# Windowed attention and SwiGLU on one core: attention after the first tile by four heads, in array quadrants

## The chip, the cores and the metric

The kernel runs on one core of a Trainium2 chip. A core has a TensorE (PE, matmuls), a VectorE (DVE), a ScalarE (ACT), a GpSimd (POOL) and a SyncE (SP); the last issues DMAs, and GpSimd and ScalarE issue some too. The metric is the device time of one execution in microseconds, the median of several. A profile is one execution more, taken with the hardware profiler; its span runs from the first instruction to the last.

## The reference

Eight batches of eight heads, 576 positions, 64 elements a head. Each position attends to itself and the 63 before it. The result, 4608 tokens of 512, goes through a SwiGLU block of width 1536.

```python
scores = scale * np.matmul(q, k.transpose(0, 1, 3, 2))        # scale = 1/8
rel = pos[:, None] - pos[None, :]
mask = (rel >= 0) & (rel < 64)
attn = softmax(np.where(mask, scores, -1e9))
x = np.matmul(attn, v)            # heads side by side: (4608, 512)
g = x @ w_gate
out = (g / (1 + np.exp(-g)) * (x @ w_val)) @ w_out
```

Inputs and the output are float32; the kernel computes in bfloat16 with float32 sums.

## The kernel before

**Tiles.** Nine tiles of 512 tokens. Tiles 0 to 6 and 8 are the first 512 positions of a batch; tile 7 (`LAST`) collects the last 64 positions of all eight batches. In a tile of the first kind the keys fall into eight blocks of 64, and a block of 64 queries needs two of them: its own and the one before. In tile 7 each batch has one block of queries and two blocks of keys.

**Pairs.** A pair `u` is two heads. `qT` and `kT` hold a pair's transposed queries and keys, 64 partitions a head, four pairs in four slots. `scores` computes keys by queries: for key block `j`, one matmul per head, 64 deep (a head's elements), 64 wide (the block's keys), over the queries of blocks `j` and `j + 1`, 128 columns. The result goes to partitions 64 (j mod 2) and on of `s_ps`, so even and odd key blocks lie in two partition halves of 512 columns, one PSUM bank a head. Queries of block 0 have no block before; a matmul with the tile `zero` fills that place. ScalarE takes the exponential of 128 x 1024 into `E`, and VectorE multiplies with a 0/1 mask. (In tile 0 a bias matmul in the accumulation does the masking.)

`totals` multiplies `E` with ones, 128 deep, so that both key halves are summed, a head on each column half. ScalarE forms the reciprocal as exp(-ln(sum)). `mix` multiplies with v: per query block and head one matmul, 128 deep (both key blocks), 64 wide, over 64 columns. For that v must exist in two arrangements, since a query block's two key blocks stand in the two halves in either order: `v1` as loaded and `v2`, shifted by 64 positions. The shift is done by VectorE for tiles 0 and 1 (`shift_pair`) and by DMAs of SyncE after that (`shift_v` with `shift_dma`). `scale` multiplies with the reciprocal into `xT`.

**The loop.** For each tile `t` from 2 on, TensorE's order, which is the order of the code, is: scores of pairs 0 and 1; the output projection of rows `s = 0` of the tile before; scores of pairs 2 and 3; sums of pairs 0 and 1; projections 1 and 2; sums of pairs 2 and 3; all products (`mix_all`); projection 3; then twelve SwiGLU blocks (`gate_value`), 8 matmuls of 128 x 128 x 512 each. A projection is 12 matmuls of that size. Tile 1 does its attention between the columns of tile 0's projection (`columns`). VectorE transposes the next tile's queries and keys between the blocks (`turn`, with L192 and L202), in order with the products of the SwiGLU blocks (L326).

**PSUM.** Two double-bank buffers (`ps_a`) hold scores, then attention outputs; two banks `g` and two banks `v` (`ps_f`) hold gates and values, projections (`g`) and sums (`v`).

**Loads.** GpSimd's queue brings weights and, two tiles ahead, queries and keys with a cast to bfloat16 (`load_qk`: four loads `q_s`, sixteen `k_s`, L87 and L107). v comes over SyncE as float32 (`stage_v`, four DMAs, one buffer) and GpSimd casts it (`cast_v`, L148); for tiles 1 and 2 GpSimd's queue loads it with the cast (L128). A load on GpSimd's queue waits until the one eight before it has landed; SyncE's DMAs have eight such places too. GpSimd's order around tile 1 is: a third of the gate weights, `q_s` of tile 1, two thirds of `wo`, four loads of v, the last third of `wo`, and the loads of tile 2. SyncE stores the output rows (`project_end`), then shifts v, then loads the next float32 v.

Of the kernel before, what the change touches and what calls it, by code (L numbers as in the profile page):

```python
# [8 lines left out]
P = 128  # L9
# [8 lines left out]
def kernel(  # L18
# [22 lines left out]
    epool = ctx.enter_context(tc.tile_pool(name="epool", bufs=7))  # L41
# [9 lines left out]
    v1 = [cst.tile([P, 4, H, D], BF16, name=f"v1{i}") for i in range(2)]  # L51
    v2 = [cst.tile([P, 4, H, D], BF16, name=f"v2{i}") for i in range(2)]
# [3 lines left out]
    zero = cst.tile([P, 64], BF16, name="zero")  # L56
    bias = cst.tile([P, 2, 4, 4, 2, 16], BF16, name="bias")
    mask = cst.tile([P, 2, 16, 4, 2, 4], BF16, name="mask")
    maskl = cst.tile([P, 2, 16, 8, 4], BF16, name="maskl")
# [66 lines left out]
    def load_v(eng, dst, t, which=range(4)):  # L126
        for i in which:
            eng.dma_start(  # L128
                dst[:, i], v[batch(t), :, P * i:P * i + P].rearrange("h r d -> r h d")
            )  # L130

    def load_last_v():
        for b in range(8):
            nc.gpsimd.dma_start(
                (v1, v2)[b // 4][LAST % 2][:, b % 4],
                v[b, :, S - P:S].rearrange("h r d -> r h d"),
            )

    def new_v(t):
        staged[t, "v"] = stage.tile([P, 4, H, D], FP32, name="v_f", tag="v", bufs=1)  # L140

    def stage_v(t):
        new_v(t)
        load_v(nc.sync, staged[t, "v"], t)

    def cast_v(t, which=range(4), copy=nc.gpsimd.tensor_copy):
        for i in which:
            copy(v1[t % 2][:, i], staged[t, "v"][:, i])  # L148

    def shift_pair(t, u):  # L150
        hs = slice(2 * u, 2 * u + 2)
        a, b = v1[t % 2][:, :, hs], v2[t % 2][:, :, hs]
        nc.vector.tensor_copy(b[64:128, 1:4], a[64:128, 0:3])
        nc.vector.tensor_copy(b[0:64], a[0:64])

    def shift_v(t, copy, lo=0, hi=4):

        a, b = v1[t % 2], v2[t % 2]
        top = min(hi, 3)
        if top > lo:  # L160
            copy(b[64:128, lo + 1:top + 1], a[64:128, lo:top])
        copy(b[0:64, lo:hi], a[0:64, lo:hi])
# [44 lines left out]
    def scores(t, u):  # L207

        qT = queries[t][:, u, :]
        E = epool.tile([P, 2, 512], BF16, name="E", tag="E")  # L210
        s_ps = ps_a.tile([P, 2, 512], FP32, name="s_ps", tag="a")
        if t == LAST:
            pieces = [
                (c, b, b + 1, kT[t % 2 if b < 4 else 2], P * (b % 4) + 64 * c)
                for b in range(8) for c in range(2)
            ]
        else:
            pieces = [(1, 0, 1, None, 0)] + [
                (j % 2, j, min(8, j + 2), kT[t % 2], 64 * j) for j in range(8)
            ]  # L220
        if t < TURNED:
            for c in range(2):
                for h in range(2):
                    r = slice(64 * h, 64 * h + 64)
                    nc.tensor.matmul(
                        s_ps[64 * c:64 * c + 64, h], identb[r, r],
                        bias[r, c ^ h].rearrange("r e i c x -> r (e i c x)"),
                        start=True, stop=False,
                    )
        for c, lo, hi, src, x in pieces:  # L230
            for h in range(2):
                r = slice(64 * h, 64 * h + 64)
                nc.tensor.matmul(  # L233
                    blocks(s_ps[64 * c:64 * c + 64, h], t, lo, hi),
                    zero[r] if src is None else src[r, u, x:x + 64],
                    blocks(qT[r], t, lo, hi),
                    start=t >= TURNED, stop=t >= TURNED or (lo > 5 and src is not None),
                )
        nc.scalar.activation(E[:], s_ps[:], AF.Exp, scale=0.125)  # L239
        if t >= TURNED:  # L240
            nc.vector.tensor_mul(  # L241
                E[:].rearrange("r h x -> r (h x)"),
                E[:].rearrange("r h x -> r (h x)"),
                maskl[:].rearrange("r h e b x -> r (h e b x)") if t == LAST
                else mask[:].rearrange("r h e i c x -> r (h e i c x)"),
            )
        weights[t, u] = E

    def totals(t, u, d_ps):
        for h in range(2):  # L250
            nc.tensor.matmul(  # L251
                d_ps[64 * h:64 * h + 64], ones[:, 0:D], weights[t, u][:, h, :]
            )

# [9 lines left out]
    def sums(t, u, d_ps):  # L264
        totals(t, u, d_ps)
        r = room(1)[:, 0]
        log(r, d_ps)
        invert(r)
        inverse[t, u] = r

    def mix(t, u, o_ps):
        E = weights.pop((t, u))
        for m in range(8):
            for h in range(2):
                nc.tensor.matmul(  # L275
                    blocks(o_ps[64 * h:64 * h + 64], t, m, m + 1),
                    (v1, v2)[m // 4][t % 2][:, m % 4, 2 * u + h, :] if t == LAST
                    else (v2, v1)[m % 2][t % 2][:, m // 2, 2 * u + h, :],
                    blocks(E[:, h, :], t, m, m + 1),
                )  # L280

# [5 lines left out]
    def values(t, u, o_ps):  # L287
        mix(t, u, o_ps)
        scale(t, u, o_ps)
# [7 lines left out]
    def finish_values(t):  # L297
        for u in (2, 3):
            sums(t, u, d_tile())
        mix_all(t)  # L300

    def mix_all(t):
        tiles = wide("ao_ps"), wide("ao_ps")
        for u in range(4):
            mix(t, u, tiles[u // 2][:, u % 2])
        for u in range(4):
            scale(t, u, tiles[u // 2][:, u % 2])
# [86 lines left out]
    new_v(0)  # L394
# [4 lines left out]
    load_v(nc.sync, staged[0, "v"], 0, (0, 1))  # L399
# [4 lines left out]
    nc.vector.memset(zero[:], 0.0)  # L404
    for i in range(2):
        nc.vector.memset(v2[i][64:128, 0], 0.0)
# [10 lines left out]
    for a in range(2):  # L417
        half = tri[64 * a:64 * a + 64]
        nc.gpsimd.affine_select(
            out=half[:, 1 - a], in_=half[:, 1 - a], compare_op=ALU.is_ge, fill=0.0,  # L420
            base=-1, pattern=[[-1, 64]], channel_multiplier=1,
        )
        nc.gpsimd.affine_select(
            out=half[:, a], in_=half[:, a], compare_op=ALU.is_ge, fill=0.0,
            base=0, pattern=[[1, 64]], channel_multiplier=-1,
        )
# [45 lines left out]
    load_v(nc.gpsimd, v1[0], 0, (2, 3))  # L472
    keep_warm(1)
    scores(0, 0)
# [4 lines left out]
    scores(0, 1)  # L479
# [17 lines left out]
    load_v(nc.gpsimd, v1[1], 1)  # L497
    weights_o(8, 12)
    cast_v(0, (0, 1), on_v)
    scores(0, 2)  # L500
    turn_pe(3)
    d_ps, r = wide("d_ps"), room(2)
    for u in range(2):
        totals(0, u, d_ps[:, u])
        inverse[0, u] = r[:, u]
    log(r, d_ps[:])
    invert(r)
    scores(0, 3)

    def log_of(u):  # L510
        d_ps = one("d_ps")
        totals(0, u, d_ps)
        inverse[0, u] = room(1)[:, 0]
        log(inverse[0, u], d_ps)
# [3 lines left out]
    for u in range(2):  # L518
        shift_pair(0, u)
    for u in range(2):  # L520
        values(0, u, ps_f.tile([P, 512], FP32, name="ao_ps", tag="gv"[u])[:])
    for u in (2, 3):
        shift_pair(0, u)
# [7 lines left out]
    for u in (2, 3):  # L531
        values(0, u, one("ao_ps"))
# [3 lines left out]
    for m in range(12):  # L536
# [4 lines left out]
        if m == 2:  # L541
            for i in range(4):
                nc.vector.tensor_copy(
                    mask[:, 0, :, i], tri[:].rearrange("r c (x e) -> r e c x", e=16)
                )
            nc.vector.memset(mask[64:128, 0, :, 0, 0, :], 0.0)
            nc.vector.tensor_copy(mask[:, 1], mask[:, 0])
# [18 lines left out]
    for u in range(4):  # L566
        scores(1, u)
        if u == 1:
            columns(0, 4)
    columns(4, 7)  # L570
    for u in (0, 2):
        d_ps, r = wide("d_ps"), room(2)
        for i in range(2):
            totals(1, u + i, d_ps[:, i])
            inverse[1, u + i] = r[:, i]
        log(r, d_ps[:])
        invert(r)
    load_qk(2)
    load_v(nc.gpsimd, v1[0], 2)
    for u in range(4):  # L580
        shift_pair(1, u)
# [6 lines left out]
    for t in range(1, NT):  # L588
        if t > 1:
            set_exp()  # L590
            for u in range(4):
                scores(t, u)
                if u == 1:
                    project(t - 1, 0)
            for u in range(2):
                sums(t, u, d_tile())
            for s in (1, 2):
                project(t - 1, s)
            finish_values(t)
# [4 lines left out]
        elif t + 1 < NT:  # L604
            if t > 1:
                cast_v(t + 1)
            shift_v(t + 1, shift_dma)
# [4 lines left out]
        if t == 2:  # L612
# [4 lines left out]
            for b in range(8):  # L617
                nc.gpsimd.tensor_copy(
                    maskl[:, 0, :, b], tri[:, 1].rearrange("r (x e) -> r e x", e=16)
                )  # L620
            nc.gpsimd.tensor_copy(maskl[:, 1], maskl[:, 0])
# [39 lines left out]
```

## Time and profile before

| | |
|---|---|
| Median of 3 runs | 333.98 us (332.97 to 335.63) |
| Profiled execution | span 331.9 us, 2.0 us under that median |
| TensorE clock granted | 0.997 |
| TensorE matmuls | 2743, busy 324.5 us |
| VectorE, ScalarE, GpSimd busy | 211.3, 168.6, 139.8 us |
| exp of scores (L239) | 36 of 128 x 1024, 1020 ns each |
| mask product (L241) | 28 of 128 x 1024 bf16, 709 ns each |
| log, invert (L259, L262) | 30 each of 128 x 512, 590 and 630 ns |
| scores (L233), sums (L251), products (L275) | 704, 72 and 576 matmuls recorded |

How to read the lines below: a timeline row has the start in us from the span's first instruction, the length in us, the engine, the line of the code, the operation, output <- inputs, for a matmul rows*columns of the array that it takes, the shape of the moving operand, and the number of instructions that the row merges. What stands in brackets is how long the engine had been idle before it and what ended that. A matmul's length includes its way through the array, so neighbouring rows overlap; the distance of starts is what it costs. "POOL" rows of DMAs show the issue, not the transfer.

### The profile page before, as it was taken

The numbers are of one execution on the slowest core, as the hardware profiler recorded it, in microseconds if no ns is written. First come the engines' busy times: TensorE is split into PE (matmuls) and PEld (weight loads), VectorE is DVE, ScalarE is ACT, GpSimd is POOL, SyncE is SP. The second block draws the span as 40 slices with busy tenths as digits, with TensorE's granted clock in tenths as the row PEclk, the third lists the DMA queues.
The fourth block names the chain that finished last, engine by engine and source line by source line (L and its number), as shares of the span: only waits on it lengthen the run. The fifth ranks groups of instructions, "written<-read, shape, count | busy, mean of one in ns | idle before, by whom it ended". The sixth has DMA issues, their size and how long they took to land.

```text
span 331.9 us, 6997 instructions
## 1 busy us (share of the span) xinstructions
PE 324.5 (98%) x2743; PEld 154.6 (47%) x2743; DVE 211.3 (64%) x325; ACT 168.6 (51%) x239; POOL 139.8 (42%) x249
## 2 busy tenths in 40 slices
PE   8899999999999999999999999999999999999995
PEld 4444444444544454445444444444444544454443
DVE  5855756586576856875668566856785586754431
ACT  5855556338533853377336743565347533953310
POOL 4944535846848985457024986263200000000000
PEclk9999999999999999999999999999999999999998
DMA  7999999999999779859922999199401320010013
GB/s 258 188 196 202 203 190 201 152 192 219 185 236 179 89 136 253 140 80 218 191 58 32 171 203 140 17 199 181 97 0 41 89 55 2 24 73 33 2 34 95
DMA packets 83249, 43.59 MB, mean 131 GB/s; under 512 B 63888, under 2 KB 77968, under 8 KB 83216
## 3 DMA queue, kind: packets, MB, share of 16 engines
q0 software_dynamic: 50416, 23.08, 56.4%
q1 hardware_dynamic: 31776, 19.02, 21.0%
q10 hardware_dynamic: 1024, 1.05, 1.1%
q8 instruction: 21, 0.34, 0.4%
q14 instruction: 12, 0.10, 0.1%
HBM read 54.00 MB, written 9.44 MB: 191 GB/s over the span
## 4 chain that ended last, share of the span: by engine, by line
PE 87%; DMA 8%; POOL 3%; issue 0%; SPq 0%; DVE 0%; POOLq 0%
PE o_ps L341 28%; PE g_ps L332 25%; PE v_ps L332 25%; DMA k_r<-in_k_dram 4%; DMA wo<-in_moe_w_out_dram 3%; PE s_ps L233 3%; PE d_ps L251 3%; PE ao_ps L275 2%; DMA q_f<-in_q_dram 1%; POOL wg L166 1%; POOL wv L166 1%; PE o_ps L377 1%; POOL v L128 1%; POOL qk_b L450 0%; SPq L73 0%
## 5 line engine op out<-in xcount | busy, mean ns | idle before, releaser
L325 ACT ACTIVATE sg<-g_ps 128x512 f32<-128x512 f32 x108 | 64.4, 597 | 116.4 <-PE g_ps L332 87.7
L326 DVE TENSOR_TENSOR hT<-sg,v_ps 128x512 bf16<-128x512 f32 x108 | 74.7, 693 | 60.7 <-PE v_ps L332 57.0
L332 PE MATMUL g_ps<-xT,wg 128*128 128x512 bf16 x424 | 108.8, 379 | 0.1
L332 PE MATMUL v_ps<-xT,wv 128*128 128x512 bf16 x424 | 108.8, 379 | 0.0
L341 PE MATMUL o_ps<-wo,hT 128*128 128x512 bf16 x420 | 95.2, 380 | 0.1
L107 POOL DMA_DIRECT2D k_s<-in_k_dram x112 | 60.6, 559 | 34.2 <-DMA q_s<-in_q_dram 21.6
L332 PEld LDWEIGHTS <-wv 128*128 128x128 bf16 x424 | 41.5, 98 | 50.0
L332 PEld LDWEIGHTS <-wg 128*128 128x128 bf16 x424 | 41.3, 98 | 49.5 <-issue 0.6
L341 PEld LDWEIGHTS <-hT 128*128 128x128 bf16 x420 | 39.0, 98 | 48.0 <-issue 3.3
L239 ACT ACTIVATE E<-s_ps 128x1024 bf16<-128x1024 f32 x36 | 35.1, 1020 | 8.3 <-PE s_ps L233 8.2
L202 DVE STREAM_TRANSPOSE kT<-k_s 128x512 bf16<-128x512 bf16 x28 | 35.9, 1281 | 0.0
L259 ACT ACTIVATE r<-d_ps 128x512 f32<-128x512 f32 (+1 forms) x33 | 20.8, 629 | 16.8 <-PE d_ps L251 16.7
L241 DVE TENSOR_TENSOR E<-E,mask 128x1024 bf16<-128x1024 bf16 x28 | 19.9, 709 | 12.2 <-ACT E L239 12.2
L285 DVE TENSOR_TENSOR xT<-ao_ps,r 128x512 bf16<-128x512 f32 x36 | 22.5, 684 | 6.8 <-PE ao_ps L275 6.4
L87 POOL DMA_DIRECT2D q_s<-in_q_dram x28 | 15.2, 553 | 23.5 <-DVE qT L192 13.4
L192 DVE STREAM_TRANSPOSE qT<-q_s 128x512 bf16<-128x512 bf16 x32 | 22.4, 703 | 0.9 <-DMA q_s<-in_q_dram 0.9
L262 ACT ACTIVATE r<-r 128x512 f32<-128x512 f32 (+1 forms) x33 | 22.0, 669 | 1.0
L148 POOL CAST v<-v_f 128x512 bf16<-128x512 f32 x20 | 12.4, 636 | 18.3 <-DMA v_f<-in_v_dram 12.8
L233 PE MATMUL s_ps<-qT,kT 64*64 64x128 bf16 (+1 forms) x640 | 12.4, 211 | 0.2
L387 ACT ACT_TABLE_LOAD x9 | 11.5, 1283 | 2.0 <-issue 1.9
L94 POOL DMA_DIRECT2D q_s<-in_q_dram x16 | 8.6, 628 | 9.4 <-DVE qT L192 9.4
L251 PE MATMUL d_ps<-E,ones 128*64 128x512 bf16 x72 | 11.4, 390 | 0.8 <-ACT E L239 0.8
(102 smaller groups left out, 186.9 us busy)
## 6 DMA issues: line engine op xcount, KB each, us to landing
q_s<-in_q_dram POOLq DMA_DIRECT2D x28, 248.0 KB, 7.1
k_s<-in_k_dram POOLq DMA_DIRECT2D x112, 56.0 KB, 5.1
v_f<-in_v_dram SPq DMA_DIRECT2D x22, 256.0 KB
v<-in_v_dram POOLq DMA_DIRECT2D x18, 128.0 KB, 4.8
wo<-in_moe_w_out_dram POOLq DMA_DIRECT2D x3, 512.0 KB, 12.0
v<-v SPq DMA_DIRECT2D x6, 256.0 KB
v<-v SPq DMA_DIRECT2D x6, 192.0 KB
q_f<-in_q_dram SPq DMA_DIRECT2D x4, 256.0 KB
```

The costliest lines, as they stand in the source:

```text
L107: nc.gpsimd.dma_start(k_s[p0:p0 + 32, g, :, 0:w], k[b, a:H:2, s:s + P].rearrange("u (r e) d -> r u (e d)", e=4) [:, :, 32 * c:32 * c + w],)
L192: nc.vector.transpose(queries[t][:, u, :].rearrange("r (e x) -> r e x", e=16), staged[t][0][:, u].rearrange("r (e d) -> r e d", d=D)[:, :, ...
L202: nc.vector.transpose(dst[:, u, :].rearrange("r (g x e) -> r g e x", g=4, e=4), k_s[:, :, u].rearrange("r g (e d) -> r g e d", d=D)[:, :, ...
L233: nc.tensor.matmul(blocks(s_ps[64 * c:64 * c + 64, h], t, lo, hi), zero[r] if src is None else src[r, u, x:x + 64], blocks(qT[r], t, lo, h ...
L239: nc.scalar.activation(E[:], s_ps[:], AF.Exp, scale=0.125)
L251: nc.tensor.matmul(d_ps[64 * h:64 * h + 64], ones[:, 0:D], weights[t, u][:, h, :])
L262: nc.scalar.activation(r, r, AF.Exp, scale=-1.0)
L285: nc.vector.tensor_mul(xT[t][:, u, :], o_ps, inverse.pop((t, u)))
L325: nc.scalar.activation(sg[:], g_ps[:], AF.Silu)
L326: nc.vector.tensor_mul(hT[t][:, m, :], sg[:], v_ps[:])
L332: nc.tensor.matmul(ps[:], w[:, c, P * m:P * m + P], xT[t][:, c, :], start=(c == 0), stop=(c == 3),)
L341: nc.tensor.matmul(o_ps[:], hT[t][:, c, P * s:P * s + P], wo[:, c, :], start=(c == 0), stop=(c == 11),)
```

## The change

From tile 1 on, attention works on four heads at a time (two pairs, `w`), and the arrangement of scores is another one. The line numbers of the changed kernel are shifted against those above.

- Scores: the two pairs of `w` go to the two partition halves, the two heads of a pair to two double-bank buffers. Key block `j` with queries of blocks `j` and `j + 1` gives 128 columns at 128 j, so the own block and the following block of queries stand in one row of 15 (tile 7: 16) blocks of 64. No zero matmul. Four matmuls, one for each quadrant of 64 x 64 of the array, follow one another.
- The exponentials go into fixed buffers `eb` with one more block of 64 columns in front that stays zero; exp and mask work on 960 columns (tile 7: 1024).
- VectorE then adds, for each query block, its two key blocks into `both` (128 x 512). `totals` sums over 64 rows of `both` in place of 128 of `E`, a matmul per quadrant.
- `mix` multiplies 64 deep and 64 wide over 128 columns, and accumulates the two key blocks of a query block in PSUM, even blocks first. In tile 7 the two key blocks of a batch are two matmuls of 64 columns.
- v is needed once, unshifted, with the pairs on partition halves: `load_halves`, eight loads of 64 partitions. `shift_v` is gone. For tile 7 there are sixteen loads into the old `v1`, `v2`.
- In the loop, projection 1 is split: five of its matmuls go ahead of the second scores, then the sums of the first half, then the other seven and projection 2, the sums of the second half, products, projection 3.
- The mask is built new in tile 0 (L543 to L547 before); the second mask of tile 7 is gone. Tile 0's attention is as before without the zero matmul.

```diff
-    v1 = [cst.tile([P, 4, H, D], BF16, name=f"v1{i}") for i in range(2)]
-    v2 = [cst.tile([P, 4, H, D], BF16, name=f"v2{i}") for i in range(2)]
+    v12 = cst.tile([P, 2, 4, H, D], BF16, name="v12")
+    v1, v2 = v12[:, 0], v12[:, 1]
+    vl = v12[:].rearrange("r g i (c w h) d -> r (g i) c w h d", c=2, w=2)
+    vb = [cst.tile([P, 8, 2, 2, D], BF16, name=f"vb{i}") for i in range(2)]
+    eb = [cst.tile([P, 17, 64], BF16, name=f"eb{i}") for i in range(4)]
...
+    def load_halves(eng, dst, t):
+        for hd in range(H):
+            w, x, h = hd // 4, hd // 2 % 2, hd % 2
+            eng.dma_start(
+                dst[64 * x:64 * x + 64, :, w, h],
+                v[batch(t), hd, 0:512].rearrange("(j r) d -> r j d", r=64),
+            )
...
+    def scores(t, w):
+        qT = queries[t]
+        s_ps = [wide("s_ps") for _ in range(2)]
+        for j in range(8):
...
+                pieces = [(j, min(8, j + 2), 0, kT[t % 2], 64 * j)]
+            for lo, hi, c, src, k0 in pieces:
+                for h in range(2):
+                    for x in range(2):
+                        slot = s_ps[h][half(x)].rearrange("r a b -> r (a b)")
+                        n = hi - lo
+                        o = P * j + 64 * c
+                        nc.tensor.matmul(
+                            slot[:, o:o + 64 * n].rearrange("r (n e y) -> r e n y", n=n, e=16),
+                            src[half(h), 2 * w + x, k0:k0 + 64],
+                            blocks(qT[half(h), 2 * w + x], t, lo, hi).rearrange(
+                                "r e (n y) -> r e n y", n=n),
+                        )
+        n = 1024 if t == LAST else 960
+        for h in range(2):
+            E = eb[2 * w + h]
+            flat = E[:].rearrange("r s z -> r (s z)")[:, 64:64 + n]
+            nc.scalar.activation(
+                flat, s_ps[h][:].rearrange("r a b -> r (a b)")[:, 0:n], AF.Exp, scale=0.125)
+            nc.vector.tensor_mul(
+                flat, flat, mask[:].rearrange("r j c e y -> r (j c e y)")[:, 0:n])
+            both = epool.tile([P, 8, 64], BF16, name="both", tag="both")
+            lo = 2 if t == LAST else 0
+            nc.vector.tensor_add(both[:], E[:, 1:17:2], E[:, lo:lo + 15:2])
+            weights[t, w, h] = E, both
...
+    def totals(t, w, d):
+        for h in range(2):
+            for x in range(2):
+                nc.tensor.matmul(
+                    d[x][half(h)].rearrange("r (e j y) -> r j e y", e=16, j=8),
+                    ones[half(x), 0:D],
+                    weights[t, w, h][1][half(x)].rearrange("r j (e y) -> r j e y", e=16),
+                )
...
+    def mix(t, w, o):
+        E = [weights.pop((t, w, h))[0] for h in range(2)]
+        for j in range(8) if t == LAST else (0, 2, 4, 6, 1, 3, 5, 7):
...
+                pieces = [(j, min(8, j + 2), 2 * j + 1, vb[t % 2][:, j])]
+            for lo, hi, s0, src in pieces:
+                n = hi - lo
+                for h in range(2):
+                    for x in range(2):
+                        nc.tensor.matmul(
+                            blocks(o[x][half(h)], t, lo, hi).rearrange("r e (n y) -> r n e y", n=n),
+                            src[half(x), w, h],
+                            E[h][half(x), s0:s0 + n].rearrange("r n (e y) -> r n e y", e=16),
+                            start=lo == 0 and s0 == 1, stop=lo == 7 and (t != LAST or s0 == 16),
+                        )
...
-    load_v(nc.gpsimd, v1[1], 1)
+    load_halves(nc.gpsimd, vb[1], 1)
     weights_o(8, 12)
...
-    for u in range(4):
-        scores(1, u)
-        if u == 1:
-            columns(0, 4)
+    scores(1, 0)
+    columns(0, 4)
+    scores(1, 1)
     columns(4, 7)
...
-    load_v(nc.gpsimd, v1[0], 2)
-    for u in range(4):
-        shift_pair(1, u)
+    load_halves(nc.gpsimd, vb[0], 2)
...
-            for u in range(4):
-                scores(t, u)
-                if u == 1:
-                    project(t - 1, 0)
-            for u in range(2):
-                sums(t, u, d_tile())
-            for s in (1, 2):
-                project(t - 1, s)
-            finish_values(t)
+            scores(t, 0)
+            project(t - 1, 0)
+            o_ps = out_tile()
+            project_part(t - 1, (1,), (o_ps,), range(5))
+            scores(t, 1)
+            sums(t, 0)
+            project_part(t - 1, (1,), (o_ps,), range(5, 12))
+            project_end(t - 1, 1, o_ps)
+            project(t - 1, 2)
+            sums(t, 1)
+            mix_all(t)
             project(t - 1, 3)
         set_silu()
         if t + 1 == LAST:
             load_last_v()
-        elif t + 1 < NT:
-            if t > 1:
-                cast_v(t + 1)
-            shift_v(t + 1, shift_dma)
+        elif t + 1 < NT and t > 1:
+            cast_v(t + 1)
```

## The prediction

> **What bounds the kernel now.** I read the page's busy times first, then TensorE's timeline through one steady tile (tile 4), then the timelines of the engines that feed it there, and last the loads of the first 65 us.
>
> ```profile
> PE 324.5 (98%) x2743; PEld 154.6 (47%) x2743; DVE 211.3 (64%) x325; ACT 168.6 (51%) x239; POOL 139.8 (42%) x249
> ```
>
> TensorE is the bound: 98% of the 331.9 us span, every other engine at two thirds or less. A change counts only by what it does to TensorE's stream, unless it makes that stream wait. TensorE's timeline (start us, us, engine, line, what) through the attention of tile 4:
>
> ```profile
> 143.91 0.22 PE L233 MATMUL s_ps<-qT,zero 64*64 64x64 bf16 x2
> 143.92 0.47 PE L233 MATMUL s_ps<-qT,kT 64*64 64x128 bf16 x18
> ...
> 144.50 2.76 PE L341 MATMUL o_ps<-wo,hT 128*128 128x512 bf16 x12
> 147.20 0.22 PE L233 MATMUL s_ps<-qT,zero 64*64 64x64 bf16 x2
> ...
> 147.79 0.62 PE L251 MATMUL d_ps<-E,ones 128*64 128x512 bf16 x4
> 148.34 5.35 PE L341 MATMUL o_ps<-wo,hT 128*128 128x512 bf16 x24
> 153.63 0.62 PE L251 MATMUL d_ps<-E,ones 128*64 128x512 bf16 x4
> 154.08 1.18 PE L275 MATMUL ao_ps<-E,v 128*64 128x64 bf16 x64
> 155.19 2.76 PE L341 MATMUL o_ps<-wo,hT 128*128 128x512 bf16 x12
> 157.80 1.03 PE L332 MATMUL g_ps<-xT,wg 128*128 128x512 bf16 x4
> ```
>
> Full-width matmuls of 512 columns start every 0.216 us (24 from 148.34 to 153.52, with the switch to 153.63). The chain of waits has gate stages starting at 123.26, 157.96 and 192.65: a tile takes 34.7 us, of which its 144 full-width matmuls are 31.1. The attention's small matmuls and the switches around them are 3.6 us: scores 143.82 to 144.50 (0.69), scores and sums 147.10 to 148.34 (1.25), sums and products 153.52 to 155.19 (1.67). Each switch between full and partial array shows about 0.1 us of nothing (143.82 to 143.91). Only these 3.6 us can be gained, in eight tiles.
>
> **The change, part by part.**
>
> *Scores.* Two pairs of heads before: 32 matmuls of real blocks and 4 of zeros, 4096 columns over four quadrants of the array, 0.50 us between the switches (143.91 to about 144.41): four 128-column matmuls per 58 ns, so the quadrants do run together. After: 32 matmuls, 3840 columns, none of zeros: 0.47 us. Saved 0.03 us, twice a tile.
>
> *Sums.* Before, four matmuls of 512 columns at full depth on two column halves: 0.43 us each time, plus a switch. After, four matmuls 64 deep and 64 wide, one per quadrant, in two banks. Never run here, so bounds: 0.22 us if all four overlap, 0.43 if two do. The nearest row is the scores, the same quadrants: 0.22. The second half's scores now stand next to the first half's sums with the same array shape, so the switch between them (0.1 us) should go.
>
> *Products.* Before, 64 matmuls of 64 columns, two at a time: 154.08 to 155.19, 1.11 us. After, 64 matmuls 64 deep, 64 wide, 56 of 128 columns and 8 of 64: 15 quadrant rounds. Bounds: 0.80 us at full stream (15 x 53 ns, from 0.216 us per 512), 1.75 if only two run together (30 x 58 ns). By the score rows: 15 x 58 ns = 0.87; with the switch 0.97.
>
> The three stretches become 0.66, 0.88 (0.10 + 0.47 + 0.22 + 0.09) and 1.27 (0.11 + 0.22 + 0.85 + 0.09): 2.8 us for 3.6, **0.80 us a tile**, in tiles 2 to 6 and 8: 4.8 us.
>
> One rule speaks against small matmuls as currency. The trace's row is tile 7's scores, 64 matmuls of 64 columns in 0.64 us, 10 ns each:
>
> ```profile
> 248.00 0.71 PE L233 MATMUL s_ps<-qT,kT 64*64 64x64 bf16 x64
> 248.64 2.76 PE L341 MATMUL o_ps<-wo,hT 128*128 128x512 bf16 x12
> ```
>
> The Trainium skill, "TensorE: Matmul & The Clock Gate", section "Wait — 56ns, not 53.3ns?", states that matmul starts are never closer than about 25 ns. By it (an estimate from that page) the products alone would take 64 x 25 ns = 1.6 us, 0.75 more a tile, and the change would gain nearly nothing. The measured 10 ns decides: that floor does not hold across quadrants.
>
> *Tile 7* takes its 16 blocks of two keys apart: scores stay 64 matmuls of 64 columns per half, but products go from 64 to 128 of 64 columns, at 10 ns 1.28 us for 1.11. With 0.53 saved on sums and a switch, this tile gains 0.35.
>
> *ScalarE and VectorE in the loop.* Exps shrink from 1024 to 960 columns, masks with them (0.69 to about 0.65). Added: one bf16 add of 512 elements per mask, 32 in all. Between 0.37 us (the mask's rate) and 0.69 (the 512-element rows that read fp32); strided 64-element runs do not slow the copies of v at L154 (0.29 us for 512, like the contiguous mask copy at L547), so 0.40. What they must not delay is the first half's sums, now right behind the second half's scores:
>
> ```profile
> 145.06 1.94 ACT L239 ACTIVATE E<-s_ps 128x1024 bf16<-128x1024 f32 x2
> 146.12 0.69 DVE L241 TENSOR_TENSOR E<-E,mask 128x1024 bf16<-128x1024 bf16 x1 [0.72 <-ACT E L239]
> 147.03 0.69 DVE L241 TENSOR_TENSOR E<-E,mask 128x1024 bf16<-128x1024 bf16 x1 [0.23 <-ACT E L239]
> ```
>
> Exps end at 146.0 and 146.9; mask, add, mask, add run from 146.1 to 148.3 at 0.40 an add, to 148.9 at 0.69. TensorE reaches these sums after 12 + 5 projection matmuls (3.67 us, the cover) and the second scores, at 148.65. Cost nothing, or 0.25 a tile at the slow end. Nothing urgent is queued behind the adds: the copy of o_ps (L348) follows, and its buffer is next wanted at 150.5. The second half: ScalarE exps to 150.7, four log and invert steps to 152.9, so the two sum banks come free at 151.2 and 152.4 and TensorE asks at 153.2. The last reciprocal is done at 156.0 and scaled at 156.7; the gate matmul that reads it is due at 157.6. The cover there is products and the last projection, 3.5 us; 0.9 is left.
>
> *Loads.* 1) The shifted copies of v, eight DVE copies of 0.3 us in tile 1, GpSimd's second mask (3.5 us) and 12 DMAs are gone: all were beside TensorE, worth nothing. 2) v comes by 8 loads of half the size instead of 4 (16 for 8 before tile 7). A GpSimd issue costs 0.54 us (k_s) to 0.90 (v); at 0.72 that is 2.3 us more for tiles 1 and 2, and 4.4 for tile 7, where GpSimd later idles 9.1 us. 3) Queue order matters early, with the DMA engines full. GpSimd issues a load only once the eighth before it has landed:
>
> ```profile
> 36.63 0.75 POOL L172 DMA_DIRECT2D wo<-in_moe_w_out_dram  x1 [0.32 <-DMA q_s<-in_q_dram]
> ...
> 48.90 0.54 POOL L107 DMA_DIRECT2D k_s<-in_k_dram  x1 [2.04 <-DMA wo<-in_moe_w_out_dram]
> ```
>
> The last third of wo landed just before 48.9, and TensorE first reads it at 48.8 (47.95 + 4 x 0.216): already tight. With eight v loads ahead it is issued near 43.6 instead of 36.6. The same bytes stand before it, so at best it lands as now; at worst 12 us after issue (wo's median), 55.6. I take 0.3 us late, since the loads about it land one transfer apart. Tile 1 then keeps 0.2 of its gain. 4) SyncE's fp32 v for tile 3 waited behind the shift of tile 2:
>
> ```profile
> 69.14 10.39 SPq L128 DMA_DIRECT2D v_f<-in_v_dram  x4
> ```
>
> Now it starts near 57, right behind the stores of tile 0, and shares the engines with tile 2's keys:
>
> ```profile
> 55.87 3.74 POOL L107 DMA_DIRECT2D k_s<-in_k_dram  x7 [0.20 <-issue]
> ...
> 63.84 1.27 DVE L202 STREAM_TRANSPOSE kT<-k_s 128x512 bf16<-128x512 bf16 x1
> ```
>
> The keys' last issue is at 59.1 and VectorE transposed at 63.84 without waiting. If it must wait, the SwiGLU product of the next block stands behind it and TensorE follows when it wants that bank (block 7's value half, 53.3 + 7 x 1.73 + 0.86 = 66.3). Transpose and product take 1.9 us, so keys landing by 64.4 cost nothing. k_s lands 2.6 to 10.3 us after issue, median 5.1: 61.7 to 69.4, median 64.2. Cost 0 to 5 us; I take 0.4, near the median.
>
> *At nothing:* tile 0 loses its zero matmuls, but its scores waited for transposed keys there anyway; the new mask and four memsets add about 0.5 us of VectorE in block 2 of tile 0, where it idles about 1 us per block. Projection 1 split in two accumulates as before.
>
> **Sum.** 4.8 + 0.35 + 0.2 - 0.4 = 4.95 us off the 331.9 us span: 327.0. The median of the runs shown, 333.98, stands 2.0 above that span, so **329.0**.
>
> **Rivals.** (1) *Late data*: tile 2's keys or the last wo third land 2 to 3 us later than I take, or the adds run at 0.69 (0.25 x 7 = 1.8). For it: full DMA engines, both margins under 1 us. Against: the median landing. 331.3 (330.4 to 333.5). (2) *The shorter stage meets ScalarE*: it has 11.3 us of work in a stage of 14.0 (a table load, 4 exps, 8 log/invert steps, another load), now 13.2; if exps and sums queue up, the freed time comes back as waits: 333.5. Against it: the schedule above leaves 0.7 us or more at each hand-over. (3) *Slower*: the merged quadrants overlap only in twos, because each column half now writes two accumulators at once. Products 1.75 for 0.87, sums 0.43 for 0.22, twice: 1.3 us a tile over seven tiles, 1.7 in tile 7: 10.8 in all, 339.8. It decides from a round of four above 86 ns (half of the way from 58 to 117). Against it: score rounds write four such places already, at 58 ns.
>
> **Chances.** Forecast 0.60 (327.0 to 330.4), rival 1 0.20, rival 2 0.10, rival 3 0.10. The range takes in the first two: 327.0 to 333.5. About 1% (3.3 us) is what a measurement of this kernel tells from no change, the bound being 330.6: faster 0.62, same 0.26, slower 0.12.
>
> **What would show it.** TensorE's three stretches near 0.66, 0.88 and 1.27 us; gate stages 33.9 us apart; sums directly behind scores; rounds of four products at 58 ns. Wrong would be: an idle TensorE before sums with the add as releaser, a VectorE wait on k_s near 64 us, a wait on wo near 49, or products near 1.75 us.

## The result, and the profile after

The changed kernel takes **330.5 us** (330.19 to 330.93, four runs) against 333.7 us of the kernel before (332.97 to 335.63, four runs on the same chip). The ratio is 0.990, with a 95% interval of 0.9875 to 0.9931: a gain of about 1%. The span of the profiled execution fell from 331.9 to 328.5 us, by 3.45; the prediction had 4.95. Two later series of the same kernel gave 0.9932 (0.9914 to 0.9950) and 0.9924 (0.9909 to 0.9940). The spread of times is about as wide as the differences between several of the variants below, so those are read from the profiles, in two figures: where TensorE waits, and how far apart the SwiGLU stages of neighbouring tiles start.

The page of the changed kernel, busy times first, then two groups (line, engine, operation, output <- inputs, count | busy us, mean ns | idle before):

```profile
PE 319.1 (97%) x2743; PEld 151.3 (46%) x2743; DVE 220.7 (67%) x352; ACT 167.1 (51%) x239; POOL 143.5 (44%) x256
...
L277 DVE TENSOR_TENSOR eb<-eb,mask 128x960 bf16<-128x960 bf16 (+1 forms) x32 | 21.6, 675 | 14.3 <-ACT eb L274 14.2
...
L282 DVE TENSOR_TENSOR both<-eb 128x512 bf16<-128x512 bf16 x32 | 13.9, 434 | 1.1
```

TensorE is still the bound and has 5.4 us less work. VectorE has 9.4 us more, above all the 32 adds at 0.434 us. TensorE's timeline through the attention of tile 4 (start us, us, engine, line, what):

```profile
143.72 0.38 PE L401 MATMUL v_ps<-xT,wv 128*128 128x512 bf16 x1
144.03 0.62 PE L261 MATMUL s_ps<-qT,kT 64*64 64x128 bf16 x32
144.58 3.84 PE L410 MATMUL o_ps<-wo,hT 128*128 128x512 bf16 x17
148.36 0.62 PE L261 MATMUL s_ps<-qT,kT 64*64 64x128 bf16 x32
148.80 0.39 PE L294 MATMUL d_ps<-both,ones 64*64 64x512 bf16 x4
149.12 4.27 PE L410 MATMUL o_ps<-wo,hT 128*128 128x512 bf16 x19
153.33 0.41 PE L294 MATMUL d_ps<-both,ones 64*64 64x512 bf16 x4
153.57 1.01 PE L347 MATMUL ao_ps<-eb,vb 64*64 64x128 bf16 x64
154.51 2.76 PE L410 MATMUL o_ps<-wo,hT 128*128 128x512 bf16 x12
```

A full-width matmul still takes 0.216 us from start to start, so the three stretches of small matmuls are 143.94 to 144.58 (0.64), 148.25 to 149.12 (0.87) and 153.22 to 154.51 (1.29): 2.80 us, 0.80 less than before. Sums stand directly behind scores, with no switch between them. The products run from 153.57 to 154.51; less the switch of 0.09 these are 15 rounds at 57 ns, so all four quadrants run together.

Starts of the SwiGLU stages (first gate matmul), from TensorE's timeline, and their distances:

| | tile 1 starts at | 1 to 2 | 2 to 3 | 3 to 4 | 4 to 5, 5 to 6 | 6 to 7 | 7 to 8 | span |
|---|---|---|---|---|---|---|---|---|
| before | 53.70 | 34.70 | 34.69 | 34.70 | 34.69 | 34.80 | 34.69 | 331.9 |
| changed | 54.27 | 35.06 | 33.89 | 33.89 | 33.89 | 34.42 | 33.90 | 328.5 |

A step holds the attention of the later of its two tiles. The steady step is 0.80 us shorter, tile 7's 0.38. What is missing is all in two places: tile 1 starts 0.57 later instead of 0.2 earlier (0.77 lost), and the step to tile 2 is 0.36 longer, where 0.80 less 0.4 was to be gained (0.76 lost). Together 1.5 us, which is 4.95 less 3.45. TensorE's timeline shows both as waits (in brackets: idle us and what ended it). The idle time counts from the modelled end of a matmul; by the distance of starts the two cost 0.98 and 1.17 us, and 1.17 is all that the step from tile 1 to 2 has over 33.89.

```profile
49.56 1.89 PE L410 MATMUL o_ps<-wo,hT 128*128 128x512 bf16 x8 [0.80 <-DMA wo<-in_moe_w_out_dram]
...
68.38 1.02 PE L401 MATMUL v_ps<-xT,wv 128*128 128x512 bf16 x4 [1.00 <-DVE hT L395]
```

The first waits for the last third of `wo`. GpSimd's timeline shows how that came to be late:

```profile
40.14 0.68 POOL L137 DMA_DIRECT2D vb<-in_v_dram  x1 [1.83 <-DMA wo<-in_moe_w_out_dram]
42.80 0.68 POOL L137 DMA_DIRECT2D vb<-in_v_dram  x1 [1.98 <-DMA wo<-in_moe_w_out_dram]
43.47 0.77 POOL L178 DMA_DIRECT2D wo<-in_moe_w_out_dram  x1
```

Two of tile 1's eight v loads stood 1.8 and 2.0 us, each until an earlier third of `wo` had landed and given its place free; the last third was issued at 43.47 (36.63 before) and landed at 49.51 (48.61 before). In the same stretch the core's DMA engines moved less: 75 GB/s from 44 to 46 us, before 184.

The second wait is for VectorE, which had itself waited for tile 2's keys, as its timeline shows:

```profile
66.50 1.31 DVE L208 STREAM_TRANSPOSE kT<-k_s 128x512 bf16<-128x512 bf16 x1 [2.02 <-issue]
67.62 1.30 DVE L395 TENSOR_TENSOR hT<-sg,v_ps 128x512 bf16<-128x512 f32 x2
```

The bracket names no releaser, but the last key load, issued at 60.55, landed at 66.32, just ahead of the transpose; before it landed at 63.09. In between SyncE now brings tile 3's float32 v (its queue's timeline):

```profile
57.15 7.68 SPq L137 DMA_DIRECT2D v_f<-in_v_dram  x8
```

### The profile page after: what moved, and what is told of

Read it like the earlier page. It is cut to its first block, busy times and chain, and to the rows that moved or that the text cites. A ratio compares the mean times of both kernels' runs of the same rounds, so it can differ in the third digit from the quotient of the medians.

```text
span 328.5 us, 7003 instructions
## 1 busy us (share of the span) xinstructions
PE 319.1 (97%) x2743; PEld 151.3 (46%) x2743; DVE 220.7 (67%) x352; ACT 167.1 (51%) x239; POOL 143.5 (44%) x256
## 3 DMA queue, kind: packets, MB, share of 16 engines
q10 hardware_dynamic: 1024, 1.05, 1.1%
## 4 chain that ended last, share of the span: by engine, by line
PE 85%; DMA 8%; DVE 2%; issue 2%; ACT 1%; POOL 1%; SPq 0%; DVEq 0%; POOLq 0%
PE g_ps L401 26%; PE v_ps L401 26%; PE o_ps L410 25%; DMA k_s<-in_k_dram 3%; DMA q_s<-in_q_dram 2%; PE s_ps L261 2%; DMA v_f<-in_v_dram 2%; PE ao_ps L347 2%; PE d_ps L294 1%; DMA k_f<-in_k_dram 1%; PE o_ps L446 1%; PE g_ps L381 1%; PE v_ps L381 1%; ACT L456 0%; PE ao_ps L330 0%
## 5 line engine op out<-in xcount | busy, mean ns | idle before, releaser
L394 ACT ACTIVATE sg<-g_ps 128x512 f32<-128x512 f32 x108 | 64.4, 597 | 115.1 <-PE g_ps L401 87.5
L274 ACT ACTIVATE eb<-s_ps 128x960 bf16<-128x960 f32 (+1 forms) x32 | 29.5, 974 | 16.3 <-PE s_ps L261 16.2
L277 DVE TENSOR_TENSOR eb<-eb,mask 128x960 bf16<-128x960 bf16 (+1 forms) x32 | 21.6, 675 | 14.3 <-ACT eb L274 14.2
L162 POOL CAST vb<-v_f 128x512 bf16<-128x512 f32 x20 | 11.9, 644 | 29.7 <-DMA v_f<-in_v_dram 21.6
L282 DVE TENSOR_TENSOR both<-eb 128x512 bf16<-128x512 bf16 x32 | 13.9, 434 | 1.1
L137 POOL DMA_DIRECT2D vb<-in_v_dram x16 | 10.9, 689 | 7.9 <-DMA wo<-in_moe_w_out_dram 3.8
```

What stands on the lines that cost most here:

```text
L274: nc.scalar.activation(flat, s_ps[h][:].rearrange("r a b -> r (a b)")[:, 0:n], AF.Exp, scale=0.125)
L277: nc.vector.tensor_mul(flat, flat, mask[:].rearrange("r j c e y -> r (j c e y)")[:, 0:n])
L394: nc.scalar.activation(sg[:], g_ps[:], AF.Silu)
```

## The experiments

The theory after this look: steady tiles gain what was worked out, and two late transfers took 1.5 us back. The first four runs test the transfers, the next three the steady tile, the last four what the first ones turned up.

### The keys and the float32 v

Run e1 loads tile 3's v only after tile 2's first keys have been transposed (VectorE touches the buffer, SyncE waits for that).

```diff
-            if t + 2 != LAST:
+            if t + 2 != LAST and t > 1:
                 stage_v(t + 2)
...
+            if t == 1 and m == turns[0]:
+                new_v(3)
+                nc.vector.memset(staged[3, "v"][:, 0, :, :, 0:1], 0.0)
+                load_halves(nc.sync, staged[3, "v"], 3)
```

> The changed kernel, but tile 3's float32 v is loaded only after VectorE has transposed tile 2's first keys (a small memset of the buffer stands between). Theory: the 1.0 us that TensorE waits at 67.4 us, because VectorE waits for tile 2's keys, comes from the early v loads sharing the DMA engines; then the keys land near 63 to 64.5 us instead of 66.3, the wait is gone or under 0.3 us, and the span falls from 328.5 to about 327.4. Rival: the keys are late because GpSimd issues them later (the last one at 60.55 us instead of 59.08); then the wait stays at 0.7 us or more and the span at 328.2 or above.

The keys landed at 63.8, although the last was issued at 60.60, as late as in the changed kernel; the wait was gone and the step from tile 1 to 2 fell to 33.89. So the cause of that wait holds, and the rival, the later issue, falls. But the span stayed at 328.6 and the time at 330.55 us (ratio 0.9909, 0.9893 to 0.9925): the step from tile 2 to 3 had become 34.95. TensorE's timeline of e1 in tile 3:

```profile
113.94 0.39 PE L294 MATMUL d_ps<-both,ones 64*64 64x512 bf16 x2
114.97 0.40 PE L294 MATMUL d_ps<-both,ones 64*64 64x512 bf16 x2 [0.65 <-DVE both L282]
```

The sums wait for VectorE's add, and VectorE's timeline tells why: masks that take 0.66 us elsewhere took 1.12 and 1.06, adds 0.71 for 0.43.

```profile
111.32 1.12 DVE L277 TENSOR_TENSOR eb<-eb,mask 128x960 bf16<-128x960 bf16 x1 [0.66 <-ACT eb L274]
112.47 0.71 DVE L282 TENSOR_TENSOR both<-eb 128x512 bf16<-128x512 bf16 x1
113.11 1.06 DVE L277 TENSOR_TENSOR eb<-eb,mask 128x960 bf16<-128x960 bf16 x1
114.20 0.71 DVE L282 TENSOR_TENSOR both<-eb 128x512 bf16<-128x512 bf16 x1
```

On GpSimd, the four casts of tile 4's v lie in that very stretch, 111.30 to 114.64. In e1's other tiles no mask or add of these shapes took longer than usual.

### The last third of the output weight

Run e2 puts it ahead of tile 1's v, and e3 does this and e1's edit together.

```diff
-    load_halves(nc.gpsimd, vb[1], 1)
     weights_o(8, 12)
+    load_halves(nc.gpsimd, vb[1], 1)
```

> The changed kernel, but the last third of wo is issued ahead of tile 1's eight v loads. Theory: the 0.80 us wait for wo at 49.56 us is gone (wo lands by 47 us), and the SwiGLU stage of tile 1 starts near 53.5 us instead of 54.27; but tile 2's keys land when the DMA engines let them, so the wait at 67 us grows by about what was gained here and the span stays at 328.3 to 328.6. Rival: the two waits are independent, and the span falls by 0.8 us to 327.7.

> Both edits of the two runs before. Theory: both waits go, 0.8 + 1.1 us, span about 326.6 us, near the 327.0 us forecast blind. Rival (the early stage is bound by the total of the loads, whatever their order): 327.4 or more.

In e2 the third landed at 45.0, the wait was gone and tile 1 started at 53.08. But tile 2's keys came later still, at 67.0, and TensorE lost more there (timeline of e2):

```profile
69.08 1.02 PE L401 MATMUL v_ps<-xT,wv 128*128 128x512 bf16 x4 [2.89 <-DVE hT L395]
```

In tile 2 an add was held up beside the casts as well (VectorE's timeline of e2; the casts ran from 81.74 to 84.01), and the sums came late by it:

```profile
81.48 2.82 DVE L282 TENSOR_TENSOR both<-eb 128x512 bf16<-128x512 bf16 x1
```

(The granted clock of that execution fell to 0.50 between 70 and 74 us, so its span is not compared.) The time was 330.44 us, 0.9917 (0.9901 to 0.9933). In e3 both waits were gone: from tile 0 to tile 1 37.20 us instead of 38.51, from 1 to 2 33.89. Yet the span was 329.1 and the time 330.37, 0.9901 (0.9884 to 0.9918). Tile 0 began 1.3 us later in this execution, and the step from 2 to 3 was 35.62, 1.7 too long. One mask there took 2.50 us, with GpSimd's casts from 111.42 to 114.14, and both pairs of matmuls of the first sums waited (VectorE's and TensorE's timelines of e3):

```profile
111.17 2.50 DVE L277 TENSOR_TENSOR eb<-eb,mask 128x960 bf16<-128x960 bf16 x1 [0.66 <-ACT eb L274]
114.47 0.40 PE L294 MATMUL d_ps<-both,ones 64*64 64x512 bf16 x2 [0.52 <-DVE both L282]
115.50 0.40 PE L294 MATMUL d_ps<-both,ones 64*64 64x512 bf16 x2 [0.62 <-DVE both L282]
```

The changed kernel itself, run once more beside these:

> The changed kernel once more, on the same chip as the three runs beside it: span 328.5 us, time 330.5 us, 0.990 of the kernel before.

It gave 331.46 us and a span of 328.4. In this execution the keys landed at 64.55, early enough for no wait at all; and again nothing was gained, for the step from tile 1 to 2 was 35.19 all the same. VectorE, in tile 2:

```profile
80.84 3.08 DVE L277 TENSOR_TENSOR eb<-eb,mask 128x960 bf16<-128x960 bf16 x1 [1.08 <-ACT eb L274]
83.96 0.42 DVE L282 TENSOR_TENSOR both<-eb 128x512 bf16<-128x512 bf16 x1
```

GpSimd beside it:

```profile
81.13 2.27 POOL L162 CAST vb<-v_f 128x512 bf16<-128x512 f32 x4
```

So the gain has two ways to go: the keys are late, or they are in time and a mask that meets the casts is felt. That became the second theory. (With late keys a mask was held as well, 1.19 us in the first profile of the changed kernel, but the wait for the keys is the whole of that longer step.)

### The steady tile

e4 leaves the adds out and sums the two key blocks in PSUM, with eight matmuls in place of four. e5 does every add twice. e6 takes projection 1 in one piece, as before.

```diff
-            both = epool.tile([P, 8, 64], BF16, name="both", tag="both")
-            nc.vector.tensor_add(both[:], E[:, 1:17:2], E[:, lo:lo + 15:2])
-            weights[t, w, h] = E, both
+            weights[t, w, h] = E, (E[:, 1:17:2], E[:, lo:lo + 15:2])
...
+        for g in range(2):
...
+                        weights[t, w, h][1][g][half(x)].rearrange("r j (e y) -> r j e y", e=16),
+                        start=g == 0, stop=g == 1,
```
```diff
-            nc.vector.tensor_add(both[:], E[:, 1:17:2], E[:, lo:lo + 15:2])
+            for _ in range(2):
+                nc.vector.tensor_add(both[:], E[:, 1:17:2], E[:, lo:lo + 15:2])
```
```diff
-            o_ps = out_tile()
-            project_part(t - 1, (1,), (o_ps,), range(5))
             scores(t, 1)
             sums(t, 0)
-            project_part(t - 1, (1,), (o_ps,), range(5, 12))
-            project_end(t - 1, 1, o_ps)
+            project(t - 1, 1)
```

> The changed kernel without VectorE's adds: sums are taken over the two key blocks separately, eight matmuls of 64 rows in place of four, accumulated. Theory: the adds cost TensorE nothing and save it 0.22 us at each sum: 0.43 us more a tile in tiles 2 to 8, tile 1's share hidden in its wait for wo, so 3.0 us more: span 331.5. Rival: the adds delay something that the trace does not show well, and without them part of this comes back: span under 330.5.

> The changed kernel with each of VectorE's adds done twice (0.34 us more from start to start, 0.69 us before the first sums of a tile). In tile 4 the adds end at 148.33 us and the sums start at 148.80, so 0.47 us are spare. Theory: TensorE waits about 0.25 us before the first sums of each of tiles 2 to 8, nothing before the second: 1.7 us more, span 330.2. Rival: the margin is larger than the trace suggests and the span stays within 0.5 us of 328.5.

> The changed kernel with projection 1 not split: the second scores and the first sums follow projection 0 at once. Theory: TensorE reaches the first sums 1.08 us earlier, near 147.7 in tile 4's times, but the adds end at 148.35: a wait of 0.65 to 0.7 us a tile, 4.7 us over seven tiles, span 333.2, so that the change would gain nothing against 331.9. Rival: the cover of projection 0 alone is enough and the span stays at 328.5.

| | steady step | against the changed kernel | span | time | ratio to before |
|---|---|---|---|---|---|
| changed | 33.89 | | 328.5 | 330.5 | 0.9903 (0.9875 to 0.9931) |
| e4, no add | 34.33 | +0.44 | 330.9 | 333.07 | 0.9996 (0.9976 to 1.0016) |
| e5, add twice | 34.41 | +0.52 | 333.9 | 335.19 | 1.0068 (1.0050 to 1.0086) |
| e6, not split | 34.57 | +0.68 | 332.5 | 334.58 | 1.0058 (1.0035 to 1.0081) |

e4: eight sums cost 0.21 us more than four, twice a tile. TensorE's timeline of e4:

```profile
149.15 0.60 PE L293 MATMUL d_ps<-eb,ones 64*64 64x512 bf16 x8
149.68 4.28 PE L410 MATMUL o_ps<-wo,hT 128*128 128x512 bf16 x19
```

The step grew by what TensorE has more to do and by nothing else, so the adds of the changed kernel cost nothing in a steady tile. Without them, and with the same early waits, the gain over the kernel before can't be told from none.

e5 shows how far that holds. In the changed kernel VectorE's chain in tile 4 is

```profile
146.19 0.66 DVE L277 TENSOR_TENSOR eb<-eb,mask 128x960 bf16<-128x960 bf16 x1 [0.67 <-ACT eb L274]
146.88 0.42 DVE L282 TENSOR_TENSOR both<-eb 128x512 bf16<-128x512 bf16 x1
147.22 0.65 DVE L277 TENSOR_TENSOR eb<-eb,mask 128x960 bf16<-128x960 bf16 x1
147.91 0.42 DVE L282 TENSOR_TENSOR both<-eb 128x512 bf16<-128x512 bf16 x1
...
151.74 0.42 DVE L282 TENSOR_TENSOR both<-eb 128x512 bf16<-128x512 bf16 x1
```

and ends at 148.33; the sums start at 148.80, so 0.47 us are to spare. (The chain of the second half ends at 152.16 and its sums start at 153.33: 1.17 to spare.) In e5 the two adds that follow a mask take 0.88 together, so the chain is 0.92 longer, and 0.92 less 0.47 is 0.45; the step grew by 0.52. What exceeds the spare time comes through in full, and the losses beside the casts follow the same sum: the first half's chain of tile 3 was 1.45 longer in e1 and 2.12 in e3, 0.98 and 1.65 over the 0.47, and those steps are 1.06 and 1.73 too long; the second half's chain of tile 2 in the second run of the changed kernel was 2.42 longer, 1.25 over the 1.17, and that step is 1.30 too long. (The rest of e5's loss, some 2 us, lies in tiles 1 and 2: tile 1 starts at 55.46, and the next step is 36.25.) e6 shows the cover from its other side. Without the five projection matmuls (1.08 us) the second pair of the first sums waits for its add, and the sums take 1.00 us, 148.41 to 149.41, in place of 0.32; 0.68 of the 0.80 is gone (TensorE's timeline of e6):

```profile
148.41 0.39 PE L294 MATMUL d_ps<-both,ones 64*64 64x512 bf16 x2
149.07 0.40 PE L294 MATMUL d_ps<-both,ones 64*64 64x512 bf16 x2 [0.27 <-DVE both L282]
```

### The casts

Run e7 moves GpSimd's casts of tiles 3's and 4's v behind the loads of tiles 4's and 5's queries and keys, so that they run in SwiGLU stages. Run e8 adds the edits of e1 and e2.

```diff
-        elif t + 1 < NT and t > 1:
+        elif t + 1 < NT and t > 3:
             cast_v(t + 1)
         if t + 2 < NT:
             load_qk(t + 2)
+            if t in (2, 3):
+                cast_v(t + 1)
```

> The changed kernel, with GpSimd's casts of tiles 3's and 4's v put behind the loads of the queries and keys of tiles 4 and 5 in its queue, so that they fall at about 102 and 126 us, into the SwiGLU stages, and no longer into the attention of tiles 2 and 3. Theory (the casts slow VectorE's masks and adds, and where they do the sums come late): no mask or add above 0.7 us in tiles 2 and 3, no wait of the sums; the wait for tile 2's keys stays as it falls (0 to 1.2 us), so the distance of the gate starts of tiles 1 and 2 is 33.9 to 35.1 and that of tiles 2 and 3 is 33.89; span 327.3 to 328.5. Rival (the long masks come from the loads that run in the same window, not from the casts): masks and adds of 1 to 3 us stay in one of the two tiles, where the loads are now, and the span is that of the changed kernel or longer.

> The changed kernel with the three moves together: the last third of the output weight ahead of tile 1's v, tile 3's float32 v loaded only after tile 2's first keys are turned, and the two casts out of the attention stages. Theory (1.3 us lost to the weight and its lateness, 1.2 us to the keys, and what their removal gave was eaten by the casts): tile 1's gate 37.2 us behind tile 0's, all steps between tiles 2 to 6 at 33.89, span 326.0 (328.5 less 1.3 and 1.2) to 326.6, time 328.0 to 328.6. Rival (the gain is taken by some other late datum, such as the v of tile 4, since it is loaded later): a wait of 0.5 us or more in tile 3's or 4's products, a span of 327.5 to 328.5 and a time of 329.5 to 330.5.

The casts of e7 began at 98.95 and 128.53, and all masks and adds of tiles 2 and 3 took 0.65 to 0.66 and 0.42 to 0.43. The keys landed at 65.0 without a wait, and this time the step from 1 to 2 was 33.89, as were all steady steps. The span is 327.3, although the wait for `wo` was 1.04 there. The time, 330.2 us (0.9903 to 0.9951), doesn't tell it from the changed kernel: in other executions the keys may be late as before.

e8 has no such wait left: tile 1 starts at 53.24, every steady step is 33.89, span 326.3. TensorE's timeline of e8 where the changed kernel waited for `wo`:

```profile
46.71 1.02 PE L294 MATMUL d_ps<-both,ones 64*64 64x512 bf16 x8
47.66 2.76 PE L410 MATMUL o_ps<-wo,hT 128*128 128x512 bf16 x12
50.35 1.04 PE L347 MATMUL ao_ps<-eb,vb 64*64 64x128 bf16 x64
```

Its time is **328.56 us** (328.05 to 329.16), 0.9859 of the kernel before (0.9842 to 0.9876). The changed kernel was run again beside it, on the same chip:

> The changed kernel as it is, on the same chip as its three variants: span 328.4 to 328.5, with either the wait for tile 2's keys (about 1 us) or late sums in tile 2 (about 1 us), as the loads fall; time 330.4 to 331.5.

It gave 330.90 us, 0.9924 (0.9909 to 0.9940), with a wait of 0.89 for `wo` and 1.62 for the keys; the intervals don't touch. So e8 beats both kernels, and in its profile neither a late datum nor a cast took anything.

The last run asks whether casts always slow the masks. It ties them to the end of the first mask in tiles 2 to 5 and 7, so that they run beside the second mask and the adds, and takes them out of their old place.

```diff
+            if w == 0 and h == 0 and t > 1 and t + 1 < NT and t + 1 != LAST:
+                mark = epool.tile([1, 64], BF16, name="mark", tag="mark")
+                nc.gpsimd.tensor_copy(mark[:], E[0:1, 1])
+                cast_v(t + 1)
...
-        elif t + 1 < NT and t > 1:
-            cast_v(t + 1)
```

> The changed kernel with each cast of v (tiles 3, 4, 5, 6 and 8) tied to the end of the first mask of the tile before, by a copy of 64 numbers that reads that mask's output on GpSimd, so that four casts of 0.6 us run beside the add, the mask and the add that follow. Theory (casts slow the masks and adds): in tiles 2 to 5 and 7 the second mask takes 1.1 to 3.1 us instead of 0.66 and the sums wait 0.5 to 2 us; the steps of these tiles become 34.4 to 36, the span 331 to 339. Rival (the long masks were chance, or come from the loads): masks stay at 0.66 and adds at 0.43, the steps stay at 33.89 and the span within 1 us of the changed kernel's.

The sizes expected by the theory did not come. In tile 2 the casts began only at 81.51, after the first half's masks, and a mask of the second half that came while they ran took 2.17 us. That step was 35.61: most of the excess is a wait for the keys (1.17 in the bracket), and 0.4 came from the held mask. In tile 3 and later the casts came to a VectorE that was already at work (VectorE's timeline of this run, tile 2 and tile 3):

```profile
82.13 2.17 DVE L277 TENSOR_TENSOR eb<-eb,mask 128x960 bf16<-128x960 bf16 x1 [1.08 <-ACT eb L274]
...
113.62 0.69 DVE L277 TENSOR_TENSOR eb<-eb,mask 128x960 bf16<-128x960 bf16 x1
114.34 0.71 DVE L286 TENSOR_TENSOR both<-eb 128x512 bf16<-128x512 bf16 x1
```

with GpSimd, in tile 3,

```profile
113.74 2.90 POOL L162 CAST vb<-v_f 128x512 bf16<-128x512 f32 x4
```

There the mask kept its time, the add took 0.28 us more, and the casts took 2.90 for 2.27. That is within the 0.47 to spare: the steps of tiles 3 to 6 are 33.89. The span is 328.7 and the time 331.1 (ratio 0.9922 to 0.9959), where the rival had them, though not for the rival's reason, since adds and one mask did slow down. So casts beside masks are a loss only when a mask or add is held for longer than the time to spare. What decides whether it is held is not shown: a mask that comes while casts run was held, but so were an add in e2 and masks in e3 and in the second run of the changed kernel that had begun about 0.25 to 0.3 us before the first cast.

## Why the prediction was right, and where not

**What bounds, and the steady tile: as worked out.** Scores, sums and products give 0.64, 0.87 and 1.29 us for 0.66, 0.88 and 1.27. The step of 0.80 us holds to the hundredth in tiles 3 to 6, tile 7 has 0.38 for 0.35. The bounds were settled by the nearest row each time: four quadrants run together in sums (153.33 to 153.57) and products, as they did in scores. The Trainium skill's least distance of about 25 ns between matmul starts ("TensorE: Matmul & The Clock Gate", section "Wait — 56ns, not 53.3ns?"), which by the prediction's estimate would have made the products 1.6 us, was rightly left: 64 of them took 0.94, and in tile 7 128 take 1.28, 10 ns each:

```profile
255.44 1.35 PE L347 MATMUL ao_ps<-eb,v 64*64 64x64 bf16 x128
256.72 1.47 PE L410 MATMUL o_ps<-wo,hT 128*128 128x512 bf16 x6
```

**The adds: as worked out.** 0.43 us for 0.40, and no cost in a steady tile (e4). The chain was expected to end between 148.3 and 148.9 and ended at 148.33.

**Loads, point 3, failed in size.** "The same bytes stand before it, so at best it lands as now", and 0.3 us late. It landed 0.9 later, and TensorE waited 0.80 in the bracket and 0.98 by the distance of starts (brackets of 0.21 to 1.04 in the other executions with this order). The issue itself came where the prediction had it, at 43.47 for 43.6. What failed is the step from the bytes to the landing. Eight half loads take eight of the queue's places where four whole ones took four, two of them stood until older weight loads had landed, and behind them the DMA engines fell to 75 GB/s for two microseconds; the bytes that stood before `wo` did not flow as before.

**Loads, point 4, had the mechanism and too small a size.** The keys were delayed by tile 3's v, as e1 shows; they landed at 66.3, 64.6 and 66.8 in three executions, and the wait was 1.00, 0 and 1.62 us in the brackets, for 0.4. It came where the prediction had placed it, at the value half of block 7. The limit of 64.4 belonged to a tile 1 that starts at 53.3; with a start 1.0 us later it moves to 65.4, and keys at 65.0 cost nothing in e7.

**A term was missing.** Where the keys were in time, GpSimd's casts met the masks and took 1.1 to 1.7 us instead (e1, the second run of the changed kernel, e3). The prediction let VectorE's chain run beside GpSimd as if the two had nothing in common, and gave that no price. With point 3 and point 4 sized as measured, the forecast of 4.95 us becomes 3.50, and 3.45 came; the missing term shows in the other executions.

e8, which has none of these three, gives the check on the sum: without the 0.3 and the 0.4 it would have been 5.65 us, a span of 326.3; e8's span is 326.3.

**The rivals.** Rival 1, late data, is what happened, at some 1 us where it took 2 to 3; 330.5 us lies 0.1 inside its band (the forecast's ends at 330.4) and at the bound of 1%. So the work of the steady tile was forecast by its mechanism, but the point, 329.0, was missed by 1.5 us, and the time lies inside the range because that took in rival 1. Rival 2 fell: TensorE waits for nothing in tiles 3 to 6, so ScalarE's work still fits. Rival 3 fell with the first row of products.

## What to carry to other kernels

Price the steady loop from the nearest rows and it can be right to a hundredth of a microsecond; then look as closely at the first tiles, where a queue's places and the load of the DMA engines decide, and count the places that loads take, not only their bytes. When a wait that you removed brings nothing, look in the next stage for what it had been hiding. When a change puts a short VectorE chain right ahead of TensorE, find out what GpSimd does beside it, and how much time the chain has to spare.

## What the runs showed of the hardware that was not expected

GpSimd's float32 to bfloat16 casts and VectorE's bfloat16 masks and adds from SBUF hold each other up. Undisturbed, a mask takes 0.66 us and a cast 0.60 to 0.65. Five masks that met casts ended 0.51 to 0.52 us after the end of a cast: in the changed kernel after the third (82.89, mask end 83.41), in its second run after the fourth (83.41 and 83.93), in its third run after the fourth (83.88 and 84.40), in e3 after the third (113.15 and 113.67), in e1 after the first (111.92 and 112.44). The add of 2.82 us in e2 ended 0.29 after the fourth (84.01 and 84.30). A cast that began while one of these masks had its turn took 1.03 to 1.07 us instead, beside an add about 0.80. VectorE's transposes and products that read PSUM kept their times beside the same casts (e7: 1.30, 0.72 and 0.69 us).

The Trainium skill, "SBUF — State Buffer", section "Who interferes with whom", describes an exclusive lock on a port pair that VectorE and GpSimd share, held for a whole instruction, with the order of issue deciding who waits. The runs agree that the two wait for each other. They differ in length: a mask waited not for one cast but for up to all four that stood in GpSimd's queue. Nor does the order of starts in the rows decide: in the second run of the changed kernel and in e3 the mask starts 0.29 and 0.25 us before the first cast (80.84 and 81.13, 111.17 and 111.42) and was still held, while in tile 3 of e10 a mask that starts 0.12 before one (113.62 and 113.74) kept its time. Why a mask came in at once, after the first cast or after the fourth stays open.
